# Attention with memory and an FFN on one core: in sequence 0, one memory product for both heads, one wide VectorE multiplication for the scaling, and the decoding of the weights placed behind the first units' exponentials

## The chip, the cores and the metric

The kernel runs on one core of one Trainium2 chip. The metric is the device time in microseconds (us) of one execution. A core has five engines that run their own instruction queues in order and meet only through semaphores: PE (TensorE, matrix products), DVE (VectorE), ACT (ScalarE), POOL (GpSimd) and SP (SyncE, which here only issues DMAs). In the profile, PE's weight loads are listed apart as PEld.

## The reference, cut to what matters

There are 8 sequences (b) of 576 positions and 8 heads of width 64. Everything is float32.

```python
scores = 1/8 * q @ k.T, causal;  a = softmax(scores);  local = a @ v
q_p = phi(q)                                   # phi(x) = max(x,0) + exp(min(x,0))
mem_out = (q_p @ M_prev) / (q_p @ z_prev + 1e-6)
x = g * mem_out + (1 - g) * local              # g = sigmoid(beta), one number per head
h = x @ w_in;  y = (h * clip(h + 3, 0, 6) / 6) @ w_out    # 4608 tokens, 512 -> 2048 -> 512
```

## The kernel before, in words

**Attention.** Heads go in pairs `p` (0 to 3), the two heads `h` of a pair sitting in partitions 0 to 63 and 64 to 127. A sequence is cut into blocks `i` of 128 query positions (block 4 has 64). One `Unit` is a sequence, a group of blocks `u`, a pair and a head: group 0 holds blocks 0 and 1, groups 1 to 3 hold blocks 2, 3 and 4. The units are numbered in the order sequence, group, pair, head, so units 0 to 7 are group 0 of sequence 0, and units 8 to 15 its block 2. A unit goes through these steps:

- `scores` (L349 in sequence 0): products of keys and queries into one of three PSUM buffers `sT`; L357 adds the causal mask.
- `reduce`: a maximum over the key blocks, on ACT for block 0 (L368, a copy) and on DVE for the others (L370), and then a maximum over the partitions on POOL (L372).
- `sub` (L378, DVE) subtracts it and so frees the `sT` buffer; `exp` (L385, ACT) follows. "Exponential k" below is L385 of unit k.
- `pv` (PE): L415 multiplies the weights with the values, which carry a column of ones, 65 columns in all. L416 multiplies phi(q) with the memory, 65 columns too (64 of `M_prev` and one of `z_prev`). In sequence 0 the memory tile `m_nat` has for every pair a 128 x 2 x 65 block that is zero where the rows of one head meet the columns of the other, so that the weight operand of L416 is the same for both heads of a pair: phi(q) of the pair, all 128 partitions.
- `combine`, when the second head of a pair is done: L438 to L440 (DVE) work out four factors per row (two heads, local and memory), L444 and L445 (ACT, four instructions of 64 columns) scale the four parts from PSUM into `x` and `y`, and L446 (DVE) adds them into 128 columns of `x`.

Sequence 0 is computed in float32 straight from what is loaded; the trace shows each of its matrix products as two records (passes). Sequences 1 to 7 are split into float16 high and low parts by ACT and DVE (L161, L162, `split`).

**FFN.** Tokens go in blocks of 256 (18 blocks). Block 0 is computed in float32 (L513 transposes `x`, L526 and L552 are the products), the others in float16 with three products for one (L531 to L533, L554 to L556). The weights arrive as 64-bit floating-point words, which are loaded as pairs of 32-bit integers and decoded to float32 in 16 jobs: `w_decode(n)`, L631 (ACT), L632 and L633 (DVE), L634 (ACT, magnitudes). Jobs 0 to 7 are `w_in`; their raw words use four buffers, so that job n + 4 is loaded (L619, SP) after L634 of job n. Job n = 0 serves the first products of L526. The float32 weights are afterwards split into float16 halves in place, one group of columns after another, before the FFN of block 1.

**What sets the order.** The program is written in the order of the units, with `at(...)` giving each piece a priority: for units it is the FFN step by which they are due, and for the first eight decode jobs it is -20 + 2n, earlier than the units beside which they are written. A planner goes through the instructions by these priorities and by its own estimate of when operands are there, and fixes one order for every engine before the program runs. On the chip every engine keeps to that order: an instruction that waits holds up all that stand behind it on its engine.

Of the kernel before, what the change touches and what calls it, by code (L numbers as in the profile page):

```python
# [12 lines left out]
F32 = mybir.dt.float32  # L13
# [4 lines left out]
AF = mybir.ActivationFunctionType  # L18
ALU = mybir.AluOpType
# [4 lines left out]
P = 128  # L24
# [9 lines left out]
X_T = 10  # L34
SPL_K = 4
W_T = [9] * 8 + [10, 10, 11, 11, 12, 12, 13, 13]
PSS, PSO = 3, 2

LOADS = ((0, 0), (3, 0), (0, 1), (0, 2), (0, 3), (2, 0), (2, 1), (1, 0), (1, 1), (2, 2), (1, 2), (1, 3), (2, 3))
# [24 lines left out]
LN_SA = float(np.log(SA))  # L64
# [3 lines left out]
def kernel(ctx, tc, qT, kT, v, mz, beta, w_in, w_out, out):  # L68
    nc = tc.nc
    PE, DVE, ACT, POOL, SP = nc.tensor, nc.vector, nc.scalar, nc.gpsimd, nc.sync  # L70
    B, NP, _, S = qT.shape
    H = 2 * NP
    D = 64
    NT, DM = out.shape
    DFF = w_in.shape[1]
    NB = 5
# [4 lines left out]
    def pool(name, bufs, **kw):  # L81
        return ctx.enter_context(tc.tile_pool(name=name, bufs=bufs, **kw))
# [6 lines left out]
    p2 = pool("p2", 2)  # L89
# [25 lines left out]
    amx = const.tile([P, B * NB], F32, name="amx")  # L115
    kst, qhl, qps, vst, raw, nat = [], [], [], [], [], []
# [23 lines left out]
    def at(step):  # L140

        tc.cur_priority = int(round(step * 1000))
# [10 lines left out]
    def abs_sum(acc, src):  # L153
        j = p1.tile([P, NB * P], mybir.dt.uint8, name="junk", tag="junk")[:, 0:src.free_size()]
        if len(src.shape) == 3:
            j = j.rearrange("p (a b) -> p a b", b=src.shape[2])
        ACT.activation(j[0:src.shape[0]], src, AF.Abs, accum_out=acc)
# [7 lines left out]
    slots = {}  # L165
# [158 lines left out]
    class Unit:  # L324
# [57 lines left out]

        def exp(self):
            a = self.a[:, 0:self.n]
            ACT.activation(a, a, AF.Exp, scale=slots[self.b, self.p]["esc"], bias=LN_SA)  # L385
            if self.b == 0:
                return
            self.ah = p2.tile([P, 512], F16, name=f"ah_{self.id}", tag="ah")
            POOL.affine_select(self.ah[:, 0:self.n], a, pattern=[[0, self.n]], compare_op=ALU.is_ge,  # L389
                               fill=0.0, base=1, channel_multiplier=0)  # L390
# [8 lines left out]
        def pv(self):  # L399
            b, p, h = self.b, self.p, self.h  # L400
            mt = mem[b]["t"]
            for i, nq, c0, _ in self.blocks:
                if h == 0:
                    if b == 0 and i in OF and i < 2:
                        o = ps_f.tile([P, 2 * TB], F32, name=f"o_{self.id}_{i}", tag="h")
                        groups[i] = o[:, 0:4 * (D + 1)].rearrange("p (h x e) -> p h x e", h=2, x=2)
                    else:
                        groups[i] = ps_o.tile([P, 2, 2, D + 1], F32, name=f"o_{self.id}_{i}", tag="o")
                g = groups[i]
                o, om = g[0:nq, h, 0, :], g[0:nq, h, 1, :]  # L410
                qs = slice(i * P, i * P + nq)
                cs = [slice(c0 + j * nq, c0 + (j + 1) * nq) for j in range(i + 1)]
                if b == 0:
                    for j in range(i + 1):
                        PE.matmul(o, self.a[:, cs[j]], nat[p]["v"][:, j, h, :], start=j == 0, stop=j == i)  # L415
                    PE.matmul(om, nat[p]["qp"][:, qs], mt[:, p, h, :], start=True, stop=True)  # L416
                    continue
                sl = slots[b, p]["sl"]
                vv = vst[sl]
                for j in range(i + 1):  # L420
                    PE.matmul(o, self.ah[:, cs[j]], vv[:, j, h, 0:D + 1], start=j == 0, stop=False)  # L421
                    PE.matmul(o[:, 0:D], self.ah[:, cs[j]], vv[:, j, h, D + 1:], start=False, stop=False)  # L422
                    PE.matmul(o, self.al[:, cs[j]], vv[:, j, h, 0:D + 1], start=False, stop=j == i)  # L423
                for x in range(2):
                    PE.matmul(om, qps[sl][:, h, qs], mt[:, x, 2 * p + h, :], start=x == 0, stop=x == 1)  # L425

        def combine(self):
            if self.h == 0:
                return
            b, p = self.b, self.p  # L430
            sd = slots[b, p]
            for i, nq, _, _ in self.blocks:
                if p == 0:
                    xtiles[b, i] = xpool.tile([P, DM], F32, name=f"x_{b}_{i}", tag="x")
                x = xtiles[b, i]
                g = groups[i]
                cf = small.tile([P, 2, 2], F32, name=f"cf_{self.id}_{i}", tag="cf")
                DVE.tensor_tensor(cf[0:nq], g[0:nq, :, :, D], sd["eps"][0:nq], op=ALU.add)  # L438
                DVE.reciprocal(cf[0:nq], cf[0:nq])
                DVE.tensor_tensor(cf[0:nq], cf[0:nq], sd["coef"][0:nq], op=ALU.mult)  # L440
                xs = x[0:nq, 2 * p * D:(2 * p + 2) * D]
                y = p2.tile([P, 2 * D], F32, name=f"y_{self.id}_{i}", tag="y")[0:nq]
                for h in range(2):
                    ACT.activation(xs[:, h * D:(h + 1) * D], g[0:nq, h, 1, 0:D], AF.Copy, scale=cf[0:nq, h, 1:2])  # L444
                    ACT.activation(y[:, h * D:(h + 1) * D], g[0:nq, h, 0, 0:D], AF.Copy, scale=cf[0:nq, h, 0:1])  # L445
                DVE.tensor_tensor(xs, xs, y, op=ALU.add)  # L446
                if p == NP - 1:
                    abs_sum(amx[0:nq, b * NB + i:b * NB + i + 1], x[0:nq])
                    done_tiles.append((b, i))

    done_tiles = []
# [4 lines left out]
    for n in range(NBLK):  # L456
        lst, t = [], n * TB
        while t < (n + 1) * TB:
            b, s = divmod(t, S)
            i, r = divmod(s, P)  # L460
            m = min(rows[i] - r, (n + 1) * TB - t)
# [145 lines left out]
    def w_raw(n):  # L607

        if n < 8:
            return W2[:, n % 4 * 4:n % 4 * 4 + 4, :].rearrange("p s f -> p (s f)")  # L610
        return raw[n % len(raw)]

    def w_load(n):
        w, c = jobs[n]
        if w == 0:
            src = w_in[(c % 4) * P:(c % 4 + 2) * P, (c // 4) * 512:(c // 4 + 1) * 512]
        else:
            src = w_out[c * P:(c + 2) * P, :]
        SP.dma_start(w_raw(n).bitcast(I64).rearrange("p (x f) -> p x f", x=2),  # L619
                     src.rearrange("(x p) f -> p x f", p=P))  # L620

    def w_decode(n):

        w, c = jobs[n]
        words = w_raw(n).bitcast(I32).rearrange("p (x f t) -> p x f t", x=2, t=2)
        lo, hi = words[:, :, :, 0], words[:, :, :, 1]
        m = (W1f, W2f)[w][:, c + 1:c + 3, :]
        d = m.bitcast(I32)


        ACT.activation(m, hi.bitcast(F32), AF.Prelu, scale=2.0 ** -112, alpha=-2.0 ** 32)  # L631
        DVE.tensor_single_scalar(d, d, 3, op=ALU.logical_shift_left)  # L632
        DVE.scalar_tensor_tensor(d, lo, 29, d, op0=ALU.logical_shift_right, op1=ALU.bitwise_or)  # L633
        ACT.activation(w_raw(n).bitcast(F32)[:, 0:1024].rearrange("p (x f) -> p x f", x=2), m, AF.Abs,  # L634
                       accum_out=(am1, am2)[w][:, c // 2:c // 2 + 1])
        ahead = 4 if n < 4 else len(raw)
        if n < 4 or n >= 8 and n + ahead < 16:
            w_load(n + ahead)
        if n == 3:
            for k in range(8, 8 + len(raw)):  # L640
                w_load(k)
# [67 lines left out]
    def w2_scale():  # L709
# [5 lines left out]
    units = [Unit(b, u, p, h) for b in range(B) for u in range(len(UNITS))  # L715
             for p in range(NP) for h in range(2)]
# [32 lines left out]
    for t in range(NU + 2):  # L749
# [29 lines left out]
        for n in range(16):  # L779
            if t == W_T[n]:  # L780
                at(DW[0] + DW[1] * n if n < 8 else DW[2] + DW[3] * (n - 8))
                w_decode(n)
# [44 lines left out]
```

## Time and profile before

| | us |
|---|---|
| median of 3 runs (lowest, highest) | 1115.28 (1114.72, 1116.04) |
| the profiled execution | 1113.7 |
| its span, first to last instruction | 1111.9 |
| busy in the span: PE / DVE / ACT / POOL | 1077.7 / 890.5 / 802.5 / 399.7 |

Each line of a timeline gives the start, the length (of a run of like instructions together), engine, line, operation, what is written and read, and in square brackets how long the engine sat idle before it and what ended that. Lengths of matrix products overlap, so the pace of PE is read from the distance between starts. A line of the windows view gives the busy time of each engine in a stretch, with the number of instructions in parentheses.

### The profile page before, as it was taken

What the parts mean: (1) busy time and instruction counts of PE and PEld (TensorE: products, weight loads), DVE (VectorE), ACT (ScalarE), POOL (GpSimd) and SP (SyncE); (2) the same over time, 40 slices, a digit from 0 to 9 for tenths busy, and PEclk for the clock granted to TensorE, in tenths of its full rate; (3) what the DMA queues carried; (4) which work ended last, traced back from release to release, by engine and by line L of the source; (5) the groups of instructions that cost most, each with busy time, mean ns of one, the idle gap of its engine ahead of it and who ended that gap; (6) DMA issues with size and microseconds to landing.
All of it is one profiled execution on the core that took longest, in us unless ns stands there. A gap on an engine that the chain in (4) does not pass through costs nothing. (4 is left out here: it accounts for less than half of the span.)

```text
span 1111.9 us, 28866 instructions
## 1 busy us (share of the span) xinstructions
PE 1077.7 (97%) x10768; PEld 795.1 (72%) x10768; DVE 890.5 (80%) x2330; ACT 802.5 (72%) x1964; POOL 399.7 (36%) x544
## 2 busy tenths in 40 slices
PE   7999999999999999999999999999999999999998
PEld 6888757677667767685768676868686868685664
DVE  5788869999799979997889886999798958792321
ACT  5788879779787878777777786778687847573322
POOL 2231223454345434544334533454244532350000
PEclk9999999999999999999999999999999999999999
DMA  8844453134423432434342341343422320101100
GB/s 255 292 143 155 124 149 88 43 85 123 113 61 98 99 112 69 114 81 112 86 115 37 104 127 52 82 101 96 106 83 58 84 51 12 40 11 29 29 11 19
DMA packets 101469, 101.41 MB, mean 91 GB/s; under 512 B 50256, under 2 KB 80976, under 8 KB 101328
## 3 DMA queue, kind: packets, MB, share of 16 engines
q1 hardware_dynamic: 101328, 99.56, 32.8%
q8 instruction: 85, 1.39, 0.5%
q14 instruction: 56, 0.46, 0.1%
HBM read 48.14 MB, written 9.44 MB: 52 GB/s over the span
## 5 line engine op out<-in xcount | busy, mean ns | idle before, releaser
L372 POOL PARTITION_ALL_REDUCE mb<-rm x256 | 249.1, 973 | 335.8 <-DVE rm L370 247.1
L531 PE MATMUL ph<-x,W 128*128 128x256 f16 x1088 | 297.3, 273 | 6.9 <-DVE r L540 4.2
L532 PE MATMUL ph<-x,W 128*128 128x256 f16 x1088 | 297.4, 273 | 0.0
L533 PE MATMUL ph<-x,W 128*128 128x256 f16 x1088 | 297.3, 273 | 0.0
L389 POOL TENSOR_SCALAR_AFFINE_SELECT ah<-a 128x384 f16<-128x384 f32 (+2 forms) x224 | 135.9, 610 | 208.6 <-ACT a L385 89.0
L554 PE MATMUL po<-W,g 128*128 128x512 f16 x544 | 206.2, 379 | 4.0 <-ACT ot L562 2.2
L556 PE MATMUL po<-W,g 128*128 128x512 f16 x544 | 206.2, 379 | 0.5 <-DVE g L542 0.4
L555 PE MATMUL po<-W,g 128*128 128x512 f16 x544 | 206.3, 379 | 0.0
L385 ACT ACTIVATE a<-a,scal 128x384 f32<-128x384 f32 (+2 forms) x224 | 141.4, 632 | 53.5 <-DVE a L378 43.9
L378 DVE TENSOR_TENSOR a<-sT,mb 128x128 f32<-128x128 f32 (+3 forms) x320 | 148.3, 479 | 19.6 <-POOL mb L372 15.2
L397 DVE TENSOR_TENSOR al<-a,ah 128x384 f16<-128x384 f32 (+2 forms) x224 | 137.2, 613 | 11.7 <-POOL ah L389 10.8
L370 DVE TENSOR_REDUCE rm<-sT 128x128 f32<-128x256 f32 (+3 forms) x256 | 135.1, 528 | 14.2 <-ACT rm L368 5.7
L539 ACT ACTIVATE r<-ph,bias_g,gsc 128x512 f32<-128x512 f32 x136 | 106.4, 782 | 34.9 <-PE ph L533 33.0
L540 DVE SCALAR_TENSOR_TENSOR r<-r,ph 128x512 f32<-128x512 f32 x136 | 91.9, 676 | 47.1 <-ACT r L539 46.7
L353 PE MATMUL sT<-slot 128*128 128x128 f16 (+1 forms) x840 | 126.3, 211 | 3.0 <-DVE a L378 3.0
L354 PE MATMUL sT<-slot 128*128 128x128 f16 (+1 forms) x840 | 127.8, 210 | 0.0
L444 ACT ACTIVATE x<-o,cf 128x64 f32<-128x64 f32 (+1 forms) x320 | 100.3, 313 | 32.4 <-DVE cf L440 25.9
L531 PEld LDWEIGHTS <-W 128*128 128x128 f16 x1088 | 106.7, 98 | 19.4 <-issue 2.3
L532 PEld LDWEIGHTS <-W 128*128 128x128 f16 x1088 | 106.6, 98 | 19.3 <-issue 4.2
L421 PE MATMUL o<-slot,ah 128*128 128x65 f16 (+1 forms) x840 | 116.2, 195 | 2.7 <-POOL ah L389 2.4
L541 ACT ACTIVATE g<-r 128x512 f16<-128x512 f32 x136 | 86.1, 634 | 44.0 <-DVE r L540 43.6
L533 PEld LDWEIGHTS <-W 128*128 128x128 f16 x1088 | 106.6, 98 | 12.2
(155 smaller groups left out, 2351.6 us busy)
## 6 DMA issues: line engine op xcount, KB each, us to landing
slot<-q SPq DMA_DIRECT2D x112, 144.0 KB, 2.5
out<-ot SPq DMA_DIRECT2D x36, 256.0 KB, 2.0
stv<-vn SPq DMA_DIRECT2D x28, 320.0 KB, 3.3
W<-w_in SPq DMA_DIRECT2D x8, 1024.0 KB, 11.3
slot<-w_out SPq DMA_DIRECT2D x8, 1024.0 KB, 5.0
stq<-qT SPq DMA_DIRECT2D x28, 288.0 KB, 3.1
stk<-kT SPq DMA_DIRECT2D x28, 288.0 KB, 3.1
slot<-k SPq DMA_DIRECT2D x112, 72.0 KB, 2.0
```

The costliest lines, as they stand in the source:

```text
L370: DVE.tensor_reduce(rm[:, m0:m0 + nq], src.rearrange("p (t q) -> p q t", q=nq), axis=AX.X, op=ALU.max)
L372: POOL.partition_all_reduce(mb[:, 0:self.m], rm[:, 0:self.m], P, RMAX)
L378: DVE.tensor_tensor(a[:, c0:c0 + w].rearrange("p (t q) -> p t q", q=nq), self.sT[:, c0:c0 + w].rearrange("p (t q) -> p t q", q=nq), self.m ...
L385: ACT.activation(a, a, AF.Exp, scale=slots[self.b, self.p]["esc"], bias=LN_SA)
L389: POOL.affine_select(self.ah[:, 0:self.n], a, pattern=[[0, self.n]], compare_op=ALU.is_ge, fill=0.0, base=1, channel_multiplier=0)
L397: DVE.tensor_tensor(self.al[:, 0:n], self.a[:, 0:n], self.ah[:, 0:n], op=ALU.subtract)
L531: PE.matmul(ph[:, m], wh, f["xh"][:, c], start=c == 0, stop=False)
L532: PE.matmul(ph[:, m], wh, f["xl"][:, c], start=False, stop=False)
L533: PE.matmul(ph[:, m], wl, f["xh"][:, c], start=False, stop=c == 3)
L554: PE.matmul(po, gh[:, m, ts], W2[:, m, 0:512], start=m == 0, stop=False)
L555: PE.matmul(po, gh[:, m, ts], W2[:, m, 512:], start=False, stop=False)
L556: PE.matmul(po, gl[:, m, ts], W2[:, m, 0:512], start=False, stop=m == 15)
```

## The change

Three things are changed; sequences 1 to 7 keep their code, but for their place in the planner's order.

1. In sequence 0 L416, one product of 65 columns for each head, becomes one product of 130 columns (`mt[:, p]`, both heads) per block and pair, issued with the second head. Its result lands in the same places of the PSUM tile, `g[0:nq, :, 1, :]`.
2. In sequence 0 the four ACT scalings (L444, L445) become one DVE multiplication of the 2 x 2 x 64 columns in PSUM with the four factors, spread over 64 columns each, into a tile `z`; the DVE addition then reads the two halves of `z`.
3. The first decode instruction of each job, L631, is to be issued on ACT after a named exponential: `W_AFTER` gives unit 3 for job 0, 4 for job 1, 5 for jobs 2 and 3, 6 for jobs 4 and 5, 7 for all others. `tc.issue_after` fixes only the order on ACT; it adds no semaphore.

```diff
+W_AFTER = [3, 4, 5, 5, 6, 6, 7, 7] + [7] * 8
...
-            ACT.activation(a, a, AF.Exp, scale=slots[self.b, self.p]["esc"], bias=LN_SA)
+            self.exp_ins = ACT.activation(a, a, AF.Exp, scale=slots[self.b, self.p]["esc"], bias=LN_SA)
...
-                    PE.matmul(om, nat[p]["qp"][:, qs], mt[:, p, h, :], start=True, stop=True)
+                    if h == 1:
+                        PE.matmul(g[0:nq, :, 1, :], nat[p]["qp"][:, qs], mt[:, p], start=True, stop=True)
...
+                if b == 0:
+                    z = p2.tile([P, 2, 2, D], F32, name=f"z_{self.id}_{i}", tag="y")[0:nq]
+                    DVE.tensor_tensor(z, g[0:nq, :, :, 0:D],
+                                      cf[0:nq].unsqueeze(3).broadcast_to([nq, 2, 2, D]), op=ALU.mult)
+                    DVE.tensor_tensor(xs.rearrange("p (h d) -> p h d", h=2), z[:, :, 0], z[:, :, 1], op=ALU.add)
+                    if p == NP - 1:
+                        abs_sum(amx[0:nq, b * NB + i:b * NB + i + 1], x[0:nq])
+                        done_tiles.append((b, i))
+                    continue
...
-        ACT.activation(m, hi.bitcast(F32), AF.Prelu, scale=2.0 ** -112, alpha=-2.0 ** 32)
+        with tc.issue_after(units[W_AFTER[n]].exp_ins.ins):
+            ACT.activation(m, hi.bitcast(F32), AF.Prelu, scale=2.0 ** -112, alpha=-2.0 ** 32)
```

## The prediction

> **What bounds the kernel now.** I read the page first, then the windows of the span one after another.
>
> ```profile
> span 1111.9 us, 28866 instructions
> ...
> PE 1077.7 (97%) x10768; PEld 795.1 (72%) x10768; DVE 890.5 (80%) x2330; ACT 802.5 (72%) x1964; POOL 399.7 (36%) x544
> ```
>
> ```profile
> 18.00:20.50 2.50, 0.07 (x1) 0.11 (x1) 2.47 (x5) 1.21 (x2) 0.00 (x0) 1.00 0.99 250
> 20.50:30.00 9.50, 9.24 (x45) 8.46 (x45) 7.02 (x23) 8.77 (x25) 3.18 (x3) 1.00 1.01 314
> 30.00:67.30 37.30, 37.30 (x160) 32.89 (x158) 29.39 (x80) 32.37 (x82) 11.64 (x12) 1.00 0.67 233
> 67.30:140.00 72.70, 72.70 (x457) 58.67 (x456) 61.10 (x146) 61.23 (x135) 17.95 (x21) 1.00 0.48 145
> 140.00:150.00 10.00, 8.52 (x66) 5.44 (x65) 3.81 (x17) 7.12 (x20) 0.90 (x2) 1.00 0.59 162
> 150.00:300.00 150.00, 144.54 (x1563) 105.18 (x1561) 137.33 (x368) 124.07 (x319) 62.01 (x84) 0.99 0.35 93
> ...
> 900.00:1050.00 150.00, 150.00 (x1521) 108.65 (x1520) 96.35 (x239) 79.25 (x182) 40.39 (x61) 1.00 0.09 21
> ```
>
> The first number after the comma is PE's busy time, then weight loads, DVE, ACT, POOL. PE has an idle hole at 18 us and none from 30 to 140 us; sequence 0's attention lies before about 155 us. From 900 us PE works off what is left of the FFN without a gap. So the end is set by the sum of PE's work and of PE's holes: whatever leaves either of them early in the span should reach the end, unless a new hole takes it. Busy is not pace, though: the stretch from 30 to 67 us holds 160 records in 37 us, the next one 457 in 73. The same products before and after 67 us:
>
> ```profile
> 33.51 1.65 PE L349 MATMUL sT<-slot 64*128 64x128 f32 x6
> 34.95 0.31 PE L357 MATMUL sT<-slot 64*128 64x64 bf16 x2
> ...
> 51.92 1.54 PE L415 MATMUL o<-slot,a 128*128 128x65 f32 x6
> 53.26 0.63 PE L416 MATMUL o<-m_nat,slot 128*128 128x65 f32 x2
> ...
> 71.32 0.71 PE L349 MATMUL sT<-slot 64*128 64x128 f32 x4
> 71.96 0.88 PE L415 MATMUL o<-slot,a 128*128 128x65 f32 x6
> 72.68 0.39 PE L416 MATMUL o<-m_nat,slot 128*128 128x65 f32 x2
> ```
>
> L415, 65 columns, takes (53.26 - 51.92) / 6 = 0.223 us a pass early and (72.68 - 71.96) / 6 = 0.12 late; L349, 128 columns, (34.95 - 33.51) / 6 = 0.24 early and (71.96 - 71.32) / 4 = 0.16 late. PE runs at about half its pace until 67 us, although the rows show a granted clock of 1.00. Almost twice the columns cost only 0.02 to 0.04 us more per pass: here the number of passes is paid, not their width.
>
> **The hole at 18 us.** Rows of ACT, DVE, POOL and PE around it:
>
> ```profile
> 13.16 0.52 ACT L385 ACTIVATE a<-a 128x384 f32<-128x384 f32 x1 [0.57 <-DVE a L378]
> 16.63 1.13 ACT L631 ACTIVATE W<-W 128x1024 f32<-128x1024 f32 x1 [2.95 <-DMA W<-w_in]
> 17.67 0.26 ACT L368 ACTIVATE rm<-sT 128x128 f32<-128x128 f32 x1
> ```
> ```profile
> 12.72 0.41 DVE L378 TENSOR_TENSOR a<-sT,mb 128x256 f32<-128x256 f32 x1
> 13.05 0.41 DVE L370 TENSOR_REDUCE rm<-sT 128x128 f32<-128x256 f32 x1
> 17.80 0.69 DVE L632 TENSOR_SCALAR W<-W 128x1024 int32<-128x1024 int32 x1 [4.33 <-ACT W L631]
> 18.52 1.23 DVE L633 SCALAR_TENSOR_TENSOR W<-W,W 128x1024 int32<-128x1024 int32 x1
> 19.66 0.61 DVE L378 TENSOR_TENSOR a<-sT,mb 128x128 f32<-128x128 f32 x2
> ```
> ```profile
> 13.55 1.06 POOL L372 PARTITION_ALL_REDUCE mb<-rm  x1 [1.27 <-DVE rm L370]
> ```
> ```profile
> 17.35 0.63 PE L416 MATMUL o<-m_nat,slot 128*128 128x65 f32 x2
> 20.43 0.76 PE L349 MATMUL sT<-slot 64*128 64x128 f32 x2 [2.44 <-DVE a L378]
> ```
>
> Job 0's L631 stands right behind exponential 1 and waits 2.95 us for its words. Behind it on ACT stands unit 3's L368. DVE stands 4.33 us at job 0's L632, and behind that L632 stands unit 2's subtraction, whose maximum POOL had by 13.55 + 1.06 = 14.61. It starts at 19.66, five microseconds late, and PE waits 2.44 us for the `sT` buffer that it frees.
>
> **The change part by part.**
>
> *The tie.* Job 0 goes behind exponential 3. The subtraction of unit 2 can then start at 14.6, before PE has finished at 18, so the hole closes: **-2.4 us**. Late next would be unit 3: its L368 no longer waits, its maximum takes POOL another 1.1 us, its exponential comes at about 17.5 to 18, and its `sT` buffer is free by then, well before PE asks for it after some four more microseconds of unit 5's scores and unit 2's L415. Job 0 behind it starts about 18, when its words (there at 16.6) are no wait any more. What hangs on the jobs: L634, then the load of job n + 4, then L526, whose first real run starts only at 63.3 us (below). Decodes shifted by a few microseconds stay under that. What I cannot exclude is that a job now stands at the head of ACT before its words are there, since attention runs ahead while the loads do not; that is the slow rival.
>
> *The product.* Per block and pair two products of two passes become one of two passes. At the early pace: 4 x 0.213 to 0.223 us go, 2 x 0.24 come (130 columns taken like the 128 of L349), 0.37 to 0.41 us less; at the later pace 4 x 0.12 - 2 x 0.16 = 0.16. Block 4 has half the weight columns:
>
> ```profile
> 128.45 0.28 PE L416 MATMUL o<-m_nat,slot 128*64 128x65 f32 x2
> 128.66 0.43 PE L349 MATMUL sT<-slot 64*128 64x64 f32 x2
> ```
>
> There a pass takes at most 0.21 / 2 us, and no row shows what 130 columns do with half a weight load; by the width they could cost all that the fewer passes save, or save half of it, 0.2: I take nothing for these four. Of the other sixteen, the eight of blocks 0 and 1 and two of block 2 are run before 67 us, six after: 10 x 0.39 + 6 x 0.16 = 4.9 us. Since PE has no hole between 30 and 140 us all of it counts: **-4.9 us** (ends 4.0 and 5.7).
>
> *The scaling.*
>
> ```profile
> L445 ACT ACTIVATE y<-o,cf 128x64 f32<-128x64 f32 x32 | 10.1, 315 | 0.0
> L444 ACT ACTIVATE x<-o,cf 128x64 f32<-128x64 f32 x32 | 9.9, 308 | 0.0
> ```
> ```profile
> 23.92 0.29 ACT L444 ACTIVATE x<-o,cf 128x64 f32<-128x64 f32 x1
> ...
> 24.70 0.29 ACT L368 ACTIVATE rm<-sT 128x128 f32<-128x128 f32 x1
> ```
>
> Four scalings hold ACT for 24.70 - 23.92 = 0.78 us, so about 20 x 0.78 = 15.6 us leave ACT (the rows above are its 64 instructions of blocks 0 to 3). The multiplication reads 256 columns of PSUM like the 128x256 subtraction above, which held DVE from 12.72 to 13.05: 20 x 0.33 = 6.6 us are added to DVE. PE waits for neither directly. ACT's share only loosens the chain. DVE's is hidden by its own idle time: from 20.5 to 140 us it is busy 7.02 + 29.39 + 61.10 = 97.5 of 119.5 us, so 22 are free; and if that cover fails, each microsecond of it can hold up a subtraction and so PE. Ends 0 and 6.6; I take **+1**, near the lower end, since PE shows no hole there now and ACT's waits in the same chain get shorter.
>
> *Sum*: -2.4 - 4.9 + 1 = -6.3, so the profiled execution's 1113.7 becomes 1107.4. The median of the runs stands 1.6 above that execution: **1109.0**.
>
> **The rivals.**
>
> *PE's pace rises earlier.* L526 before and after the turn:
>
> ```profile
> L526 PE MATMUL ph<-x,W x10: 379/634/737, 63.3 to 67.1; 128*128 128x256 f32 x10
> ...
> L526 PE MATMUL ph<-x,W x115: 379/379/483, 67.1 to 124.2; 128*128 128x256 f32 x115
> ```
> ```profile
> 45.83 0.63 PE L416 MATMUL o<-m_nat,slot 128*128 128x65 f32 x2
> ```
> ```profile
> 53.03 0.28 DVE L446 TENSOR_TENSOR x<-x,y 128x128 f32<-128x128 f32 x1
> ```
>
> The full pace came 3.8 us into the first long run of L526. That run needs `x` of blocks 0 and 1, whose last product ended near 46.3 and whose last addition came at 53.03, after queueing on ACT and DVE. If the shorter `combine` lets the run come five microseconds of work earlier, these five go at 0.12 / 0.223 of their time: 2.3 us more gain, 1106. Against it: the place of L526 on PE is fixed in the planner's order, by its own clock. The Trainium skill (TensorE: Matmul & The Clock Gate, Part 1) has it that the clock is released by some 3.4 us of sustained activity; by that, PE without the hole would run full from early on. The trace disagrees as far as it goes: PE is busy without a gap from 30 us and keeps the slow pace for 37 us. As a mechanism of this kernel: if the closed hole alone brought the full pace at 20 us, PE's 46.5 us of work up to 67.3 would shrink to some 25, but DVE's 36.4 us in the same stretch plus ten multiplications, 3.3, would then bound it at 39.7: 6.8 us more gain at most, 1102.
>
> *DVE becomes the bound.* After 150 us DVE is busy 137 of 150 us; if the same happens before, all 6.6 us come back: 1113.7 - 7.3 + 6.6 + 1.6 = 1114.6, no change. For it speaks DVE's 84% between 67 and 140 us, against it that PE waits for DVE there not once.
>
> *A decode blocks ACT (slower).*
>
> ```profile
> 31.80 7.21 SPq L619 DMA_DIRECT2D W<-w_in  x3
> ...
> W<-w_in SPq DMA_DIRECT2D x8, 1024.0 KB, 11.3
> ```
> ```profile
> 48.39 1.54 PE L415 MATMUL o<-slot,a 128*128 128x65 f32 x6
> ```
>
> The loads of `w_in` end with an issue at about 38.7 us that lands some 11 us later, near 50, and DMA is full in between, so this doesn't get earlier. The tie lets job 7 stand right behind exponential 7. If the planner puts it ahead of exponential 8, ACT stands until 50, exponential 8 ends near 52, and PE, which then could start unit 8's L415 at 48.4 - 6.5 = 42, waits 10 us, less what scores it can still put into free buffers: nothing, as all three are waiting for ACT. That is 7.3 gained, 10 lost, and about 1 for the crowd behind: 1113.7 + 3.7 + 1.6 = 1119. It decides from the point where ACT's wait at L631 exceeds 7 us in all. For it: job 0 was misjudged in just this way, by 2.95 us. Against it: jobs 2 to 7 don't wait now, and the planner is only told "not before".
>
> *The change doesn't do what it says*: the tie leaves job 0 or 1 where another subtraction stands behind it, the hole stays, and the product alone gives -4.9 + 1: 1111.4.
>
> **How the numbers follow.** Forecast 1109 (own range 1107 to 1111): 0.46. Earlier pace, 1106: 0.17; at once, 1102: 0.04. Hole stays, 1111.4: 0.08. DVE the bound, 1114.6: 0.13, a third of it with enough gain left to count as faster. ACT blocked, 1119: 0.12. A measurement of this kernel can tell about 0.2%, 2.2 us, so faster is below 1113.05 and slower above 1117.5. Faster: 0.46 + 0.17 + 0.04 + 0.08 + 0.04 less 0.03 for what a new order of everything behind may cost = 0.76; slower 0.11; same 0.13. The range from 1102 to 1115.5 leaves out the blocked case and the far ends, 0.18.
>
> **What would show each step.** Hole: the rows near 18 us, no PE idle time of over 0.5 us between 9 and 30 us. Product: 40 records fewer of the memory product, two passes of about 0.22 to 0.25 us. Scaling: a DVE row of 128x256 in sequence 0 of about 0.41 us, and ACT's busy time down by 15 to 25 us (its lengths overlap, so up to 20 x 4 x 0.31). Pace: the time at which L526's passes halve. ACT blocked: idle time before L631 that names the DMA of `w_in`. The prediction is wrong if PE's idle time in the span does not fall by about 2 us, or if new waits of PE for L378 appear between 30 and 150 us.

## The result, and the profile after

The changed kernel takes 1103.53 us (median of 4 runs, 1101.76 to 1104.74), the kernel before 1115.66 beside it: a ratio of 0.989, 95% interval 0.987 to 0.991, or 12.1 us less. The forecast was 6.3 us less. The profiled execution took 1104.08 us. Lines of the changed kernel are numbered a little higher: L349 becomes L350, L378 L379, L385 L386, L415 L416, L526 L537, L631 L643.

The page, and the windows that were shown of before:

```profile
span 1102.4 us, 28691 instructions
...
PE 1071.2 (97%) x10728; PEld 788.6 (72%) x10728; DVE 893.0 (81%) x2350; ACT 789.0 (72%) x1884; POOL 405.2 (37%) x544
```

```profile
18.00:20.50 2.50, 2.50 (x15) 2.28 (x14) 0.62 (x3) 0.00 (x0) 0.00 (x0) 1.00 0.79 227
20.50:30.00 9.50, 7.20 (x35) 6.33 (x34) 6.71 (x21) 6.51 (x14) 2.13 (x2) 1.00 1.01 316
30.00:67.30 37.30, 36.02 (x160) 31.75 (x160) 32.94 (x79) 29.04 (x60) 11.01 (x11) 1.00 0.57 207
67.30:140.00 72.70, 72.70 (x455) 56.85 (x454) 63.30 (x163) 55.51 (x102) 16.26 (x20) 1.00 0.50 152
140.00:150.00 10.00, 7.51 (x34) 3.76 (x32) 6.59 (x19) 5.05 (x10) 2.74 (x3) 0.83 0.81 189
```

The forty records of the memory product are gone, as the page's counts show, and ACT is 13.5 us less busy. But the hole did not close. The stretch from 18 to 20.5 us is full, and the next one lacks 2.3 us of PE. Up to 67.3 us PE idles more than before: (9.50 - 7.20) + (37.30 - 36.02) = 3.6 us against 2.43 + 0.26 = 2.7. Part of this is a new wait of 1.06 us at 36.50, for a subtraction whose maximum POOL had by 33.95 us and which stands on DVE behind L645 of a decode:

```profile
34.53 1.23 DVE L645 SCALAR_TENSOR_TENSOR W<-W,W 128x1024 int32<-128x1024 int32 x1
...
35.76 0.59 DVE L379 TENSOR_TENSOR a<-sT,mb 128x128 f32<-128x128 f32 x2
```
```profile
36.50 1.62 PE L350 MATMUL sT<-slot 64*128 64x128 f32 x6 [1.06 <-DVE a L379]
```

ACT, DVE and PE around the new hole:

```profile
15.25 0.52 ACT L386 ACTIVATE a<-a 128x384 f32<-128x384 f32 x1 [0.44 <-DVE a L379]
21.10 0.47 ACT L268 ACTIVATE slot<-slot 128x320 f32<-128x320 f32 x1 [5.33 <-DMA slot<-qT]
...
23.22 0.52 ACT L386 ACTIVATE a<-a 128x384 f32<-128x384 f32 x1
```
```profile
14.54 0.62 DVE L379 TENSOR_TENSOR a<-sT,mb 128x128 f32<-128x128 f32 x2 [1.19 <-POOL mb L373]
...
22.11 0.49 DVE L270 SCALAR_TENSOR_TENSOR slot<-slot 128x320 f32<-128x320 f32 x1 [3.41 <-ACT slot L269]
22.51 0.62 DVE L379 TENSOR_TENSOR a<-sT,mb 128x128 f32<-128x128 f32 x2
```
```profile
19.43 1.54 PE L416 MATMUL o<-slot,a 128*128 128x65 f32 x6
23.23 0.76 PE L350 MATMUL sT<-slot 64*128 64x128 f32 x2 [2.26 <-issue]
```

Unit 2's subtraction now runs at 14.54, as worked out (14.6). But unit 3's stands behind L270 of phi for the later columns of q, whose ACT part, L268, waits 5.33 us for its load. Before, the decode had stood there first and had covered this wait. PE asks for the buffer at 21 us and gets it at 23.2, when that subtraction has ended (PE's row names "issue"): in this execution the hole has moved by one unit and kept its size.

The size depends on when the loads land. Three of the runs below (e10, e11, e12) have the changed kernel's order up to this place. ACT stands 3.75, 3.21 and 4.46 us at L268 there, and PE waits 0.7, 0 and 1.3 us. ACT and PE of e11:

```profile
18.81 0.47 ACT L268 ACTIVATE slot<-slot 128x320 f32<-128x320 f32 x1 [3.21 <-DMA slot<-qT]
```
```profile
20.94 0.77 PE L350 MATMUL sT<-slot 64*128 64x128 f32 x2
```

The old hole varies in the same way: e8 and e9, with the order of the kernel before up to there, have 2.29 and 0.82 us where it has 2.44.

So the hole gave nothing to the 9.5 us by which the span fell. PE's idle time in the span went from 1111.9 - 1077.7 = 34.2 to 1102.4 - 1071.2 = 31.2 us; its busy time fell by 6.5, of which the merged product accounts for 4.0 (worked out below). Three stretches behind sequence 0's attention, where the two kernels run the same code, first before and then after:

```profile
160.00:200.00 40.00, 37.41 (x357) 28.80 (x356) 36.49 (x97) 33.68 (x88) 14.23 (x18) 0.96 0.28 78
...
400.00:500.00 100.00, 94.35 (x1095) 71.63 (x1093) 92.89 (x239) 78.63 (x197) 44.70 (x61) 1.00 0.31 83
...
600.00:700.00 100.00, 97.64 (x1042) 68.43 (x1040) 82.15 (x224) 75.29 (x191) 38.69 (x54) 1.00 0.37 95
```
```profile
160.00:200.00 40.00, 39.70 (x404) 30.44 (x402) 36.88 (x99) 34.73 (x87) 17.17 (x17) 1.00 0.39 109
...
400.00:500.00 100.00, 96.75 (x1146) 73.75 (x1144) 93.84 (x251) 83.21 (x210) 44.19 (x65) 1.00 0.37 87
...
600.00:700.00 100.00, 99.75 (x1075) 70.61 (x1072) 83.72 (x230) 75.57 (x192) 42.92 (x55) 1.00 0.42 106
```

In these 240 us PE idles 10.6 us before and 3.8 after. They are the three that gained most; others lost, and from 140 to 1050 us as a whole PE's idle time falls from 20.9 to 17.9 us (rows below). Nothing in the diff speaks of them. This left two theories. **A**, the steps of the prediction: the parts act in sequence 0 and add up. **B**: the planner lays out the whole program anew whenever something early changes, and the quality of that layout, hundreds of microseconds later, moves the end as much as the change does.

### The profile page after: what moved, and what is told of

It reads as the page before. It is cut to its first block, busy times and chain, and to the rows that moved or that the text cites. A ratio compares the mean times of both kernels' runs of the same rounds, so it can differ in the third digit from the quotient of the medians.

```text
span 1102.4 us, 28691 instructions
## 1 busy us (share of the span) xinstructions
PE 1071.2 (97%) x10728; PEld 788.6 (72%) x10728; DVE 893.0 (81%) x2350; ACT 789.0 (72%) x1884; POOL 405.2 (37%) x544
## 4 chain that ended last, share of the span: by engine, by line
PE 39%; DVE 18%; ACT 5%; issue 5%; DMA 4%; POOL 1%; SPq 1%; DVEq 0%; ACTq 0%; POOLq 0%
PE po L565 6%; PE po L567 6%; PE po L566 6%; PE ph L542 5%; PE ph L543 5%; PE ph L544 5%; DVE rm L371 3%; DVE a L379 3%; DVE al L398 3%; DVE r L551 2%; DVE g L553 2%; PE sT L354 1%; PE sT L355 1%; PE o L425 1%; PE o L423 1%
## 5 line engine op out<-in xcount | busy, mean ns | idle before, releaser
L373 POOL PARTITION_ALL_REDUCE mb<-rm x256 | 253.9, 992 | 354.5 <-DVE rm L371 249.8
L390 POOL TENSOR_SCALAR_AFFINE_SELECT ah<-a 128x384 f16<-128x384 f32 (+2 forms) x224 | 138.3, 619 | 183.0 <-ACT a L386 124.3
L386 ACT ACTIVATE a<-a,scal 128x384 f32<-128x384 f32 (+2 forms) x224 | 141.0, 631 | 63.1 <-DVE a L379 54.1
L379 DVE TENSOR_TENSOR a<-sT,mb 128x128 f32<-128x128 f32 (+3 forms) x320 | 148.3, 479 | 25.6 <-POOL mb L373 19.7
L355 PE MATMUL sT<-slot 128*128 128x128 f16 (+1 forms) x840 | 126.7, 210 | 0.0
L354 PE MATMUL sT<-slot 128*128 128x128 f16 (+1 forms) x840 | 124.2, 210 | 1.9 <-DVE a L379 1.4
L424 PE MATMUL o<-slot,ah 128*128 128x64 f16 (+1 forms) x840 | 115.2, 195 | 0.0
L455 ACT ACTIVATE x<-o,cf 128x64 f32<-128x64 f32 (+1 forms) x280 | 88.0, 314 | 37.4 <-DVE cf L442 37.2
```

The lines of the kernel that those rows point to most:

```text
L373: POOL.partition_all_reduce(mb[:, 0:self.m], rm[:, 0:self.m], P, RMAX)
L379: DVE.tensor_tensor(a[:, c0:c0 + w].rearrange("p (t q) -> p t q", q=nq), self.sT[:, c0:c0 + w].rearrange("p (t q) -> p t q", q=nq), self.m ...
L386: self.exp_ins = ACT.activation(a, a, AF.Exp, scale=slots[self.b, self.p]["esc"], bias=LN_SA)
```

## The experiments

The ratio is that to the kernel before on the same chip, with its 95% interval; idle is the span less PE's busy time on the page of the one profiled execution. e1 to e4 ran on one chip, e5 to e11 on a second, e12 on a third; the kernel before took 1115.0 to 1115.8 us beside each of them.

| kernel | median us | ratio | interval | idle us |
|---|---|---|---|---|
| before | 1115 to 1116 | 1 | | 34.2 |
| changed | 1103.5 | 0.9891 | 0.9870 to 0.9913 | 31.2 |
| e1 product alone | 1117.0 | 1.0024 | 1.0005 to 1.0042 | 38.6 |
| e2 scaling alone | 1125.3 | 1.0093 | 1.0075 to 1.0111 | 37.5 |
| e3 tie alone | 1126.2 | 1.0117 | 1.0088 to 1.0147 | 41.3 |
| e4 product and scaling | 1106.0 | 0.9916 | 0.9887 to 0.9946 | 31.2 |
| e5 product and tie | 1116.1 | 0.9999 | 0.9976 to 1.0022 | 39.2 |
| e6 changed, phi tied too | 1116.3 | 0.9990 | 0.9966 to 1.0015 | 37.9 |
| e7 changed, ten products ahead | 1122.2 | 1.0050 | 1.0034 to 1.0066 | 43.1 |
| e8 before, copy in unit 12 | 1111.8 | 0.9966 | 0.9948 to 0.9985 | 32.1 |
| e9 before, copy in unit 20 | 1112.9 | 0.9979 | 0.9965 to 0.9993 | 30.3 |
| e10 changed, copy in unit 12 | 1115.4 | 0.9998 | 0.9978 to 1.0017 | 36.8 |
| e11 changed, copy in unit 20 | 1112.8 | 0.9968 | 0.9949 to 0.9987 | 36.0 |
| e12 changed, copy in unit 40 | 1104.1 | 0.9902 | 0.9885 to 0.9918 | 30.9 |

### The parts one by one

e1 to e5 are the kernel before with the named parts of the diff and without the others; scaling with the tie was not tried.

```diff
 # e1: this part alone; e4: with the scaling; e5: with the tie
-                    PE.matmul(om, nat[p]["qp"][:, qs], mt[:, p, h, :], start=True, stop=True)
+                    if h == 1:
+                        PE.matmul(g[0:nq, :, 1, :], nat[p]["qp"][:, qs], mt[:, p], start=True, stop=True)
```

> The kernel before with the merged memory product alone. Theory A (the steps of the prediction: the parts add up and act in sequence 0): 4.9 us less than before, 1111 us, with the hole of PE near 18 us still there. Theory B (what was gained beyond the steps comes from the new order that the planner gives all later work, so the parts don't add up): any time from 1107 to 1118, with PE's last float32 scores 4 to 5 us earlier and the end not earlier by the same amount.

```diff
 # e2: this part alone
+                if b == 0:
+                    DVE.tensor_tensor(z, g[0:nq, :, :, 0:D],
+                                      cf[0:nq].unsqueeze(3).broadcast_to([nq, 2, 2, D]), op=ALU.mult)
+                    DVE.tensor_tensor(xs.rearrange("p (h d) -> p h d", h=2), z[:, :, 0], z[:, :, 1], op=ALU.add)
...
+                    continue
```

> The kernel before with the one wide VectorE multiplication alone. Theory A: 0 to 1 us slower than before, 1116 us, as PE has no hole that ACT's scalings cause. Theory B: 1110 to 1119 with the difference arising after 150 us. A third reading, that shorter work on ACT is what moved the planner to a better order, wants this part alone to bring 3 us or more.

```diff
 # e3: this part alone
+        with tc.issue_after(units[W_AFTER[n]].exp_ins.ins):
+            ACT.activation(m, hi.bitcast(F32), AF.Prelu, scale=2.0 ** -112, alpha=-2.0 ** 32)
```

> The kernel before with the decodes tied behind the exponentials alone. Theory A as predicted (the hole at 18 us closes): 2.4 us less than before, 1113 us. What the profile of the changed kernel suggests instead (the hole is only handed to the next early wait of ACT, for q's later columns): 0 to 1 us less, with a hole of over 2 us near 20 us and ACT's idle time before L267 naming a DMA. Theory B: 1110 to 1119.

> The changed kernel without the tie: merged product and wide multiplication. Theory A: the sum of the two alone, about 1111 to 1112 us. If the tie is worth nothing because its hole moves on, this runs like the changed kernel, 1103 to 1105 us. Theory B: neither; the sum of the single parts' differences misses by more than 3 us.

> The changed kernel with ACT's four scalings in place of the wide multiplication. Theory A: 4.9 + 2.4 us less than before, 1108 us, a little faster than the changed kernel if the multiplication costs DVE time that counts. If the multiplication is what carried the extra gain: 1108 us or more, 4 us slower than the changed kernel. Theory B (order): 1103 to 1113, not the sum of the single parts.

Theory A falls at once. By the ratios the single parts cost 0.2, 0.9 and 1.2% (about 3, 10 and 13 us), yet product and scaling together gain 0.8%, and all three gain 1.1%. Theory B's ranges were too narrow as well: e2 and e3 lie above 1119 us, e5 above 1113. To product and scaling the tie adds nothing that can be told apart (0.9916 and 0.9891, with overlapping intervals), nor to the product (1.0024 and 0.9999); alone it costs 1.2%.

What e3 was expected to show, a hole of PE handed on to phi, did not come. ACT's wait is there, but on DVE unit 3's subtraction (the first L379 row below) stands ahead of phi's L270 in this order, and PE has no hole. ACT, DVE and PE of e3:

```profile
19.89 0.47 ACT L268 ACTIVATE slot<-slot 128x320 f32<-128x320 f32 x1 [4.15 <-DMA slot<-qT]
```
```profile
18.71 0.41 DVE L379 TENSOR_TENSOR a<-sT,mb 128x256 f32<-128x256 f32 x1
...
21.57 0.49 DVE L270 SCALAR_TENSOR_TENSOR slot<-slot 128x320 f32<-128x320 f32 x1
```
```profile
22.19 0.79 PE L350 MATMUL sT<-slot 64*128 64x128 f32 x2
```
```profile
9.00:30.00 21.00, 20.26 (x98) 18.54 (x96) 11.93 (x37) 12.92 (x37) 5.32 (x5) 1.00 1.02 331
```

Between 9 and 30 us PE idles 21 - 20.26 = 0.7 us, where the kernel before idles 3.0. In e3, then, the tie alone did at its place what the prediction wanted of it, and yet the end is some 12 us later. The loss is late. In the first 140 us e3 idles no more than before (6.4 against 7.5 us). From 140 to 1050 us, in before, e3, e5 and the changed kernel:

```profile
140.00:1050.00 910.00, 889.12 (x9691) 648.59 (x9690) 770.38 (x2010) 676.52 (x1686) 362.20 (x496) 1.00 0.31 80
```
```profile
140.00:1050.00 910.00, 880.93 (x9561) 637.24 (x9560) 760.67 (x1992) 671.56 (x1670) 366.62 (x495) 1.00 0.31 79
```
```profile
140.00:1050.00 910.00, 885.48 (x9635) 644.81 (x9635) 764.97 (x2001) 671.37 (x1676) 367.41 (x496) 0.99 0.32 79
```
```profile
140.00:1050.00 910.00, 892.05 (x9706) 650.26 (x9704) 768.65 (x2012) 677.64 (x1676) 369.97 (x497) 1.00 0.32 81
```

PE idles 20.9, 29.1, 24.5 and 17.9 us there. Apart from the end of sequence 0's attention, up to about 160 us, no part of the change touches this stretch except through the layout.

Idle time is not the whole loss: e2 idles less than e1 and e5 and ends later, as its PE is busy for 1085.0 us. Part of such busy time is run at half the clock. In e2 this happens three times behind the early stretch, from 159.4, 418.8 and 538.3 us on; the first of them:

```profile
159.42:166.24 6.82, 6.07 (x17) 2.97 (x15) 6.09 (x23) 5.13 (x14) 2.37 (x4) 0.50 0.07 9
```

With 3.4 us each for the other two these are 13.6 us, as in e1 and e5; before and changed have one stretch of 3.4 us, e12 none until its last microseconds. How much of each kernel's time goes back to this is open.

### Closing the hole for good

e6 issues phi of the later columns behind exponentials 4 to 7 as well, and writes it later in the program.

```diff
+PHI_AFTER = (4, 5, 6, 7)
...
+        with ExitStack() as order:
+            if part == 1:
+                order.enter_context(tc.issue_after(units[PHI_AFTER[p]].exp_ins.ins))
+            ACT.activation(e, q, AF.Relu, scale=-1.0)
+            ACT.activation(e, e, AF.Exp, scale=-1.0)
...
-            if t == B_T[p]:
+            if t == PHI_AFTER[p] + 2:
```

> The changed kernel, in which phi of q's later columns (blocks 2 to 4), too, is issued on ACT behind exponentials 4 to 7. Reading of the hole near 21 us: ACT stands 5.3 us at that phi for its DMA and holds up unit 4's L369. If so, PE's hole of 2.3 us before 23.2 us goes and the end is 2 us earlier, about 1101.5 us, unless the next early wait takes it over. Theory B: the end moves by another amount, 1099 to 1107.

PE and ACT of e6 (the lower row is unit 3's exponential, here L390):

```profile
19.35 1.54 PE L420 MATMUL o<-slot,a 128*128 128x65 f32 x6
20.82 0.79 PE L354 MATMUL sT<-slot 64*128 64x128 f32 x2
```
```profile
19.23 0.52 ACT L390 ACTIVATE a<-a 128x384 f32<-128x384 f32 x1 [2.36 <-DVE a L383]
```

The scores that came at 23.23 come at 20.82 with no idle time ahead: both ties together do what the prediction wanted of one. How much of the 2.4 us the second tie brought is open, since in e11 the same scores come at 20.94 without it. The end is nevertheless 1% later than the changed kernel's (0.9990 against 0.9891), outside both expectations, and the layout idles 37.9 us in all.

### The slow pace

e7 puts ten dense products into PE's first idle microseconds.

```diff
+    wz = p1.tile([P, 512], BF16, name="wz", tag="wz")
+    POOL.memset(wz, 0.5)
+    wp = ps_f.tile([P, 2 * TB], F32, name="wp", tag="h")
+    for k in range(10):
+        PE.matmul(wp, wz[:, 0:P], wz, start=True, stop=True)
     for x, n in LOADS:
```

> The changed kernel with ten products of 128x512 bf16 of a constant tile ahead of the first scores, their result unread, in PE's idle first 4.6 us. Rival of the prediction (the slow pace until 67 us is a state that dense work ends): passes of 65 columns at 0.11 to 0.12 us from about 5 to 9 us on, and 7 us or more off the end, 1097 us or less, as far as DVE lets it. If the pace of the first 67 us is set by something else (operands, float32 weight loads), passes stay at 0.21 to 0.22 us and the end is unchanged or up to 1 us later.

PE's timeline, and windows of e7 (the third number from the right is the granted clock):

```profile
2.46 3.68 PE L707 MATMUL wp<-wz 128*128 128x512 bf16 x10 [2.46 <-POOL wz L704]
6.07 0.49 PE L350 MATMUL sT<-slot 64*128 64x128 f32 x4
6.39 0.22 PE L358 MATMUL sT<-slot 64*128 64x64 bf16 x2
...
13.98 0.76 PE L350 MATMUL sT<-slot 64*128 64x128 f32 x2 [5.71 <-DVE a L379]
```
```profile
5.00:12.00 7.00, 3.28 (x35) 2.38 (x33) 2.77 (x16) 2.13 (x7) 0.42 (x1) 1.00 0.76 180
12.00:20.00 8.00, 6.02 (x29) 5.49 (x30) 2.86 (x9) 2.30 (x6) 2.79 (x3) 0.50 1.02 356
...
60.00:70.10 10.10, 10.10 (x45) 9.16 (x46) 9.98 (x29) 9.22 (x20) 3.63 (x6) 0.50 0.48 175
70.10:80.00 9.90, 9.90 (x68) 8.77 (x67) 8.64 (x17) 9.54 (x16) 1.15 (x2) 1.00 0.64 217
```

The changed kernel's own first scores, for the pace:

```profile
5.25 1.36 PE L350 MATMUL sT<-slot 64*128 64x128 f32 x6
6.25 0.48 PE L358 MATMUL sT<-slot 64*128 64x64 bf16 x4
```

The dense products do raise it: the first scores run at (6.39 - 6.07) / 4 = 0.08 us a record in e7, at (6.25 - 5.25) / 6 = 0.17 in the changed kernel. Then a new layout leaves PE idle for 5.71 us, the clock falls to half, and it stays there to 70 us although PE is busy almost throughout, mostly with narrow float32 products. So the slow pace of e7 is a granted clock of 0.50. The changed kernel's rows show 1.00 at the same pace (0.76 us for the two records at 23.23 there as at 13.98 here), so there the half clock is inferred from the pace. Whether PE would have kept the full clock without the 5.71 us hole is open: the run was to tell it, and the hole came in between. Neither expected time holds (1097 us or less; unchanged or up to 1 us later): e7 takes some 18 us more than the changed kernel.

### The layout alone

e8 to e12 add one copy of one column (128x1) on DVE, which nobody reads. The copy takes 0.14 us. It changes no other work; the four runs with it in unit 12 or 20 have another order on every engine from about there on. In unit 40 of the changed kernel the order of all other instructions stays the same on all engines: that is the control.

```diff
+    spare = const.tile([P, 1], F32, name="spare")
     for t in range(NU + 2):
+        if t == 12:                      # e9, e11: 20; e12: 40
+            at(due(t))
+            DVE.tensor_copy(spare, units[t - 1].mb[:, 0:1])
```

> The kernel before with one added VectorE copy of one column (128x1, a spare tile that nobody reads) in unit 12; its own cost is below 0.1 us, but the planner gives all engines another order from there on. If the order alone moves the end by many microseconds: the time differs from the kernel before by 3 us or more in either direction. If the order matters little and the parts of the change have effects of their own: 1114 to 1117 us.

> The same copy in unit 20 of the kernel before. Order theory: a third time, again 3 us or more away from at least one of the other two. Otherwise 1114 to 1117 us.

> The same copy in unit 12 of the changed kernel. Order theory: 1105 to 1118, since 1103.5 was a good draw; the mean of the changed kernels less that of the kernels before is then the change's own worth, 3 to 6 us by sequence 0. If the change itself is worth 12 us: 1102 to 1105 us.

> The same copy in unit 20 of the changed kernel. Order theory: another time between 1105 and 1118. If the change itself is worth 12 us: 1102 to 1105 us.

> The same copy in unit 40 of the changed kernel, where the planner's order of all other instructions stays as it is in the changed kernel, on every engine. Order theory: 1102 to 1106 us, like the changed kernel, since it is the order and not the copy that moved the time by 9 to 12 us in units 12 and 20. If the copy itself costs it, or the changed kernel's first runs were a lucky chip: 1110 us or more.

With a new layout the changed kernel loses its gain: 0.9998 in e10 and 0.9968 in e11, 9 to 12 us slower than in its own layout. With its own layout and the same copy it keeps it, 0.9902 in e12. So the copy is not the cost; what e10 and e11 have beyond it is another order. Two reservations stand. The changed kernel itself was not run on the chip of e10 and e11, so an effect of that chip on this kernel alone is not excluded. And one order has no one time: the ten executions of e10 range from 1108.6 to 1117.7 us. The kernel before moves less, by -0.3% and -0.2%, here on the same chip. Its expectation of 3 us holds for e8 (3.2) and not for e9, which is 2.1 us from before and 1.1 from e8.

Over three layouts each, the mean ratio of before is (1 + 0.9966 + 0.9979) / 3 = 0.9982, that of the changed kernel (0.9891 + 0.9998 + 0.9968) / 3 = 0.9952. The difference is 0.3%, 3 us, and with a spread of 0.6% within the second three it is not told from zero. Taking all layouts with the merged product but e7 and the control (changed, e1, e4, e5, e6, e10, e11: mean 0.9969) against all without it (before, e2, e3, e8, e9: mean 1.0031), the product is worth 0.6%, about 7 us, with an uncertainty of some 4 us (one standard error) from these spreads. That fits the 4.0 us worked out below, but doesn't show it.

## Why the prediction was right in sign and range, and where its steps failed

**What bounds the kernel.** "The end is set by the sum of PE's work and of PE's holes" held as far as it went: the three fastest kernels (changed, e4, e12) idle 31 us, the three slowest (e2, e3, e7) 37 to 43; e9, with 30.3 us of idle time and 1112.9 us, has PE busy for longer. What I did not draw from it: 20.9 of the 34.2 us of holes lie between 140 and 1050 us, and they change with the layout.

**The hole, -2.4 us: failed in the changed kernel.** The step "unit 3 ... its L368 no longer waits ..., its exponential comes at about 17.5 to 18" passed over phi's later columns, L268 to L270, which stand in ACT's and DVE's order between unit 2 and unit 3 and whose loads land at about 21 us. The exponential came at 23.22, and the subtraction ahead of it, which frees the buffer, at 22.51. In e3's order that subtraction is ahead of phi, and the hole closes. I followed the chain of one unit's own steps and not what else is queued on the two engines it runs through; the loads of the later columns were in the code (`B_T`). e6 shows that with this second wait out of the way the hole does close, though the exponential still comes only at 19.23, behind a wait for DVE. I also took the size of both holes from one execution, and they vary with the loads, by 1.6 us in the old one (e9) and 2.3 in the new one (e11). And I added this term to the next one, though a shorter product brings PE to the buffer sooner: at 21.0 in the changed kernel, at 22.2 in e3.

**The product, -4.9 us: the lower end.** Passes of 130 columns, early and late, in the changed kernel:

```profile
15.52 0.74 PE L418 MATMUL o<-m_nat,slot 128*128 128x130 f32 x2
16.06 0.95 PE L416 MATMUL o<-slot,a 128*128 128x65 f32 x4
...
69.28 0.44 PE L418 MATMUL o<-m_nat,slot 128*128 128x130 f32 x2
69.65 0.20 PE L358 MATMUL sT<-slot 64*128 64x64 bf16 x1
```

(16.06 - 15.52) / 2 = 0.27 us a pass early and (69.65 - 69.28) / 2 = 0.185 late, where I had taken 0.24 and 0.16 from the 128 columns of L349. The saving is then 10 x (4 x 0.218 - 0.54) + 6 x (4 x 0.12 - 0.37) = 4.0 us, the lower of the two ends. The four of block 4, for which I had taken nothing, have rows at 134.30 (L418) and 134.62 (the next L350): 0.16 us a pass, so about 0.1 us less each than four passes of 0.105.

**The scaling, +1 us: the duration was right, the effect on the end can't be seen.**

```profile
L446 DVE TENSOR_TENSOR z<-o,cf x20: 391/416/426, 16.9 to 159.6; 128x256 f32<-128x256 f32 x16, 64x256 f32<-64x256 f32 x4
```

The median is 0.416 us where 0.41 was taken. ACT's busy time fell by 13.5 us, somewhat less than the 15 to 25 given as a sign. PE idles nowhere between 67.3 and 140 us, so the rival in which DVE becomes the bound did not come about in this layout.

**The signs of being wrong.** PE's idle time fell by 3.0 us, as asked, but all of that behind 140 us and not in the hole. The other sign did appear: PE waits for L379 (the L378 of before) 1.06 us at 36.50 and 0.6 us at 140.84, where the kernel before has no such wait.

**The sum.** Corrected for the two terms it would be 0 - 4.0 + 1 = -3 us. The span of the profiled executions, for which it was worked out, fell by 9.5, the median by 12.1. The missing 6.5 us of the span are 3.0 of idle time, 6.5 - 4.0 = 2.5 of PE's busy time beyond the product, and the 1.0 that I charged for the scaling. No row makes any of these the work of one of my steps. The nearest thing that the prediction had is "0.03 for what a new order of everything behind may cost", a chance where a price with both signs was due: e8 and e9 put a new layout at 2 to 3 us in the kernel before, e10 and e11 at 9 to 12 in the changed one. The sign and the range were right in the layout that was drawn, and that was luck: in e10 the same change would have counted as no change.

**The rivals.** *Earlier pace*: L537 of the changed kernel.

```profile
L537 PE MATMUL ph<-x,W x20: 379/379/634, 60.8 to 65.9; 128*128 128x256 f32 x20
...
L537 PE MATMUL ph<-x,W x105: 379/379/483, 65.9 to 126.8; 128*128 128x256 f32 x105
```

The median of the run that starts at 60.8 is already the short 379 ns: the turn comes at about 63 us, some 4 us earlier than before. That is no more than the run itself moved (63.3 to 60.8) plus 1.6. That the place is the planner's to choose shows in e10, where these records of L537 give the turn at 52 us:

```profile
L537 PE MATMUL ph<-x,W x4: 571/634/793, 48.3 to 51.6; 128*128 128x256 f32 x4
...
L537 PE MATMUL ph<-x,W x36: 379/379/571, 51.6 to 67.0; 128*128 128x256 f32 x36
```

Eleven microseconds earlier than in the changed kernel, and yet e10 ends later. *The full pace at once*: refuted, since in e6, whose PE has no wait over 0.3 us between 9 and 30 us, six records of L354 from 28.63 to 30.07 still take 0.24 us each. *A decode blocks ACT*: not here; what blocked ACT at its head was a load for phi, while a decode held DVE, and with it PE, at 36 us. *The hole stays*: in substance this is what happened, at another instruction.

## What to carry to other kernels

Where a planner lays out the whole program from estimates, a small early change is measured together with a new layout of everything behind it: here one idle copy of a column went with a shift of 2 to 3 us of 1110 in the kernel before and of 9 to 12 in the changed one, there more than any of the three edits is worth by its own rows. Before crediting an edit, time it in a few layouts (a harmless copy in different places) beside a control that keeps the layout, and keep a good layout as a find of its own. Time all of them on the same chip. And when a wait at the head of an in-order engine is taken away, look for the next instruction on that engine whose data are late, whatever piece of the program it belongs to.

## What the runs showed of the hardware that was not expected

PE's clock can fall to half without a long pause. Two neighbouring windows of the kernel before:

```profile
172.50:176.00 3.50, 1.11 (x23) 0.77 (x20) 2.83 (x8) 2.31 (x4) 1.54 (x2) 1.00 0.32 98
176.00:179.40 3.40, 3.40 (x18) 2.40 (x18) 3.08 (x12) 3.40 (x10) 0.83 (x2) 0.51 0.00 0
```

No single wait here exceeded 0.9 us, yet with PE busy for 1.11 of 3.5 us the clock is granted at 0.51 for the next 3.4 us, for 18 records of dense products. By 3.4 x (1 - 0.51) this cluster of short holes cost about 1.7 us beside its own length. The Trainium skill (TensorE: Matmul & The Clock Gate, "Why this matters for your kernels") warns of idle gaps of over some 3 us between bursts; this trace shows the fall without one. In the other direction, e7 was busy with narrow float32 products for almost all of 20 to 70 us at a granted 0.50, so PE's being busy was not enough to lift the clock there; behind ten 128x512 bf16 products, 3.6 us of them, the first scores ran at the short pace. What share of wide products is needed stays open: in e10 the pace rose at 52 us with two pairs of 256-column records in the four microseconds ahead of it.
